# One p load for three batches, gate constants loaded one by one, and a new order of 300 steps in an attention and mixture-of-experts kernel

## Chip, cores and metric

The kernel runs on one core of a Trainium2 chip. The metric is the device time of one execution in microseconds (us). The kernel before takes 265.82 us, the median of three runs (265.61 to 266.9).

Engine names: PE does matmuls and transposes, PEld its weight loads, DVE is the vector engine, ACT the scalar engine, POOL the general one, SP the engine that issues DMA transfers (its own waits show as SPq). Each engine takes its instructions in the order in which the program lists them.

## What is computed

The reference is a chain of three stages on float32 data (4 batches, 8 heads, 576 rows, head dimension 64, 32 packed rows, 8 experts), cut here to what matters:

```python
def sm_attn(qq, kk, vv):                  # softmax(qq kk^T / 8) vv
    ...
p_packed = sm_attn(p, k, v)               # 32 rows per head attend to 576
out = sm_attn(q, p_packed, p_packed)      # 576 rows per head attend to 32
x = out.transpose(0, 2, 1, 3).reshape(2304, 512)

# MoE 1: top-1 expert by argmax(x @ w_gate), at most `capacity` = 576 rows for one expert, in row order
#   y = gate_w * (relu(x @ w1[e]) @ w2[e]) for rows that are kept, 0 for the others
# MoE 2: the same without capacity, times sigmoid(x @ w_output_gate)[e]
```

## The kernel before

**One order written out by hand.** All of the first part, from the first load to the first layer of the second MoE, is a list of 300 steps in a string, `PLAN`. The loop `for t in PLAN.split()` near the end of the kernel reads it word by word and calls the entry of `STEPS` of that name; what a step emits goes to the end of each engine's program. So `PLAN` sets one order per engine, and through SP's order the order of the loads too. A digit after a name is a batch, a piece or a half; a last letter D, A or P names the engine that copies (DVE, ACT, POOL).

**Attention, for batches b = 0 to 3.** The steps `k`, `q` (three pieces each, L283), `v` (L276) and `p` (L265) load raw rows; `dup` (L269, on POOL) copies p beside itself, since p is needed twice along the partitions. `tk` and `tq` transpose a piece with six PE transposes (tile `tp`) and copy the result out (tile `T`, L257, on ACT). `pT` (L311) does the same for p. `sa` computes the first scores (`s<-T,pT`, through the helper of L21), `ma` their negated maximum (`nb`, L332, on DVE), `ea` the exponential with its sum (L339, on ACT). `at` transposes the result in two halves (`a1T`, copied on ACT or DVE, L259), and `pp` multiplies it with v: 144 small matmuls in two parts. `sc` scales (`pps`), `pt` transposes and copies (`ppT`). The second attention works on `ppT` and q: `sb` scores (`s<-T,ppT`), `tr` a transpose in 32 x 32 blocks on DVE (L401), `mb` maximum (L409), `su` subtraction on POOL (L413), `eb` exponential, `sm` sum and reciprocal (`dn`, L420 to L422), `mu` multiplication on POOL (L426), `bk` back into `a2T` (L429).

**First gate.** Each 576 rows of x belong to one batch, and the kernel works as if all rows of a batch chose one expert; other cases have their own code behind the plan. `gg` multiplies `ppT` with the gate's weights (`gp`), `lg` makes the logits (`lp`), `lt` transposes and sums them (`Lall`, L460). For batch 0 the chain is `oa` (`mx`, `d`, L180 to L182), `ob` (`first`, `mx`, `oh`, L187 to L190: the one-hot of the expert), `rk` (rank of each row by matmuls), `kp` (which rows are kept), `cn` (counts and the expert, L211 to L226), `ei` (the cast to an integer, L236, which SP then reads with a TENSOR_LOAD, L731). Only then can the expert's weights be loaded, `wa` for w1 (L548) and `wb` for w2 (L558), 512 KB each; SP waits at the TENSOR_LOAD, and what stands behind it in its program waits too.

**Expert of batch 0 and of batches 1 to 3.** `w` multiplies a piece of w1 with `ppT`, `xh` and `xl` split x into two parts (`xl` is L571 on POOL), `h` is one of eight chunks of the first layer, `wh` and `wl` split w2, `y` is one of 32 steps of the second layer and `yo` copies its result. `lg14`, `lt14`, `oa14`, `rk14`, `kp14`, `cn14`, `rt` and `si` are the gate of batches 1 to 3 and the choice of what the second slot works on; in the second slot the same steps run on the other batches' expert. `gl`, `gt`, `gi` and `gs` are the second MoE's gate. `cst` loads the four small constants of the gates (L131 to L134), and `prep` works on them: five POOL instructions for the capacity, and a cast and a subtraction on DVE (L143, L144) that only the second gate needs.

What follows the plan (the second slot's second layer, the second MoE) is written in plain loops and is not touched.

## Time and profile before

| | |
|---|---|
| median of three runs | 265.82 us |
| the profiled execution's own time | 266.27 us |
| its span | 264.5 us |
| PE busy | 244.8 us (93%), 2529 matmuls |
| PE's weight loads | 215.2 us (81%) |
| DVE, ACT, POOL busy | 127.3, 102.9, 49.3 us (48, 39, 19%) |
| DMA | 37.17 MB, mean 141 GB/s |

The span runs from the first to the last instruction of one profiled execution. Busy time of an engine is the time that its instructions cover; PE's weight loads overlap its matmuls. An engine's idle time has a releaser, the event that ended it; "issue" means that the profile shows no event that the engine waited for. The share of DMA is the mean busy share of the core's 16 DMA engines, and PEclk is the granted clock of PE, with 1.00 for full speed.

### The profile page before, as it was taken

The numbers are of one execution on the slowest core, as the hardware profiler recorded it, in microseconds if no ns is written. First come the engines' busy times: TensorE is split into PE (matmuls) and PEld (weight loads), VectorE is DVE, ScalarE is ACT, GpSimd is POOL, SyncE is SP. The second block draws the span as 40 slices with busy tenths as digits, with TensorE's granted clock in tenths as the row PEclk, the third lists the DMA queues.
The fourth block names the chain that finished last, engine by engine and source line by source line (L and its number), as shares of the span: only waits on it lengthen the run. The fifth ranks groups of instructions, "written<-read, shape, count | busy, mean of one in ns | idle before, by whom it ended". The sixth has DMA issues, their size and how long they took to land.

```text
span 264.5 us, 6064 instructions
## 1 busy us (share of the span) xinstructions
PE 244.8 (93%) x2529; PEld 215.2 (81%) x2529; DVE 127.3 (48%) x307; ACT 102.9 (39%) x161; POOL 49.3 (19%) x70
## 2 busy tenths in 40 slices
PE   8979674979999999999999999999999999999990
PEld 6666644756797999887999999999888999988880
DVE  0227769669886343859722253495031334621000
ACT  2858666544582204464402241263231414401110
POOL 5002337053275214311600000000020000001000
PEclk9999999799999999999999999999999999999997
...
GB/s 241 362 394 388 292 403 123 54 268 137 111 79 0 2 9 321 106 315 240 119 180 158 86 100 114 0 77 239 43 46 53 108 254 0 4 0 40 62 45 47
DMA packets 29652, 37.17 MB, mean 141 GB/s; under 512 B 4144, under 2 KB 21168, under 8 KB 29616
## 3 DMA queue, kind: packets, MB, share of 16 engines
...
q8 instruction: 22, 0.36, 0.6%
q10 hardware_dynamic: 144, 0.26, 0.3%
...
HBM read 31.25 MB, written 4.72 MB: 136 GB/s over the span
## 4 chain that ended last, share of the span: by engine, by line
PE 83%; DVE 6%; issue 4%; DMA 3%; SPq 2%; ACT 0%; POOL 0%; DVEq 0%; ACTq 0%
PE h L21 27%; PE y L21 20%; PE o L21 19%; PE tp L25 4%; PE s L21 3%; DMA v<-in_v_dram 3%; PE pp L21 3%; PE l L21 2%; PE lp L21 1%; PE ppw L21 1%; SPq L283 1%; DVE oh L190 1%; PE a1Tp L25 1%; DVE d L182 1%; DVE h L614 1%
## 5 line engine op out<-in xcount | busy, mean ns | idle before, releaser
L21 PE MATMUL o<-w2bh,h 128*128 128x512 f32 x144 | 45.9, 391 | 0.0
L21 PE MATMUL y<-h,w2ah 128*128 128x288 f32 x256 | 45.0, 297 | 0.0
L21 PEld LDWEIGHTS y<-h,w2ah 128*128 128x128 f32 x256 | 37.5, 189 | 0.9 <-issue 0.9
L614 DVE SCALAR_TENSOR_TENSOR h<-h 128x576 fp32r<-128x576 f32 (+3 forms) x64 | 25.8, 447 | 25.1 <-ACT h L607 25.1
L607 ACT ACTIVATE h<-h 128x576 fp32r<-128x576 f32 x32 | 20.8, 650 | 36.5 <-PE h L21 34.0
L21 PEld LDWEIGHTS o<-w2bh,h 128*128 128x128 f32 x144 | 26.9, 188 | 5.7
L21 PE MATMUL o<-w2bl,h 128*128 128x512 f32 x80 | 31.3, 391 | 0.0
L21 PE MATMUL h<-yh,w1bh 128*128 128x288 f32 x128 | 27.5, 296 | 0.0
L21 PE MATMUL y<-h,w2al 128*128 128x288 f32 x128 | 27.4, 295 | 0.0
L21 PE MATMUL h<-yh,w1bl 128*128 128x288 f32 x128 | 27.4, 295 | 0.0
L21 PE MATMUL h<-yl,w1bh 128*128 128x288 f32 x128 | 27.3, 295 | 0.0
L725 POOL TENSOR_SCALAR osb<-osb,g 64x512 f32<-64x512 f32 x2 | 3.2, 1577 | 109.3 <-DVE osb L724 109.3
L257 ACT ACTIVATE T<-tp 128x768 f32<-128x768 f32 x24 | 19.3, 851 | 7.9 <-PE tp L25 7.7
L526 POOL TENSOR_TENSOR w2al<-wraw,w2ah 128x1024 fp32r<-128x1024 f32 x7 | 16.6, 2390 | 26.0 <-ACT w2ah L520 26.0
L21 PEld LDWEIGHTS h<-yh,w1bh 128*128 128x128 f32 x128 | 20.6, 189 | 0.2
L21 PEld LDWEIGHTS y<-h,w2al 128*128 128x128 f32 x128 | 20.6, 189 | 0.0
L21 PEld LDWEIGHTS h<-yh,w1bl 128*128 128x128 f32 x128 | 20.6, 188 | 0.0
L21 PEld LDWEIGHTS h<-yl,w1bh 128*128 128x128 f32 x128 | 20.6, 188 | 0.0
L25 PE MATMUL tp<-ident,r 128*128 128x128 f32 x144 | 19.2, 277 | 0.8 <-DMA r<-in_k_dram 0.2
L715 ACT ACTIVATE osb<-o,g 128x512 f32<-128x512 f32 (+1 forms) x8 | 5.3, 661 | 36.9 <-PE o L21 29.0
L25 PEld LDWEIGHTS tp<-ident,r 128*128 128x128 f32 x144 | 15.9, 142 | 3.6 <-issue 1.6
L21 PEld LDWEIGHTS o<-w2bl,h 128*128 128x128 f32 x80 | 15.0, 188 | 3.3
...
## 6 DMA issues: line engine op xcount, KB each, us to landing
wraw<-in_moe_w_dram SPq DMA_DIRECT2D x32, 512.0 KB, 5.4
r<-in_k_dram SPq DMA_DIRECT2D x12, 384.0 KB, 7.3
r<-in_q_dram SPq DMA_DIRECT2D x12, 384.0 KB, 8.8
...
```

The source lines that it names most:

```text
L21: return nc.tensor.matmul(out, lhsT=lhsT, rhs=rhs, start=start, stop=stop)
L25: return nc.tensor.transpose(out, in_, ident)
L182: V.tensor_tensor(d, L, bc(mx, E), op=ALU.subtract)
L190: nc.vector.tensor_tensor(oh, rev.unsqueeze(1).to_broadcast([128, n, E]), bc(mx, E), op=ALU.is_equal)
L257: nc.scalar.activation(out=o, in_=i, func=ACTF.Copy)
L283: nc.sync.dma_start(t, (k if nm == "k" else q)[b].rearrange("h (x r) d -> (h x) r d", r=R)[:, 2 * PJ * a:2 * PJ * (a + 1), :])
L526: eng.tensor_tensor(lo, src.rearrange("p a b -> p (a b)"), hi.rearrange("p a b -> p (a b)").bitcast(FP32), op=ALU.subtract)
L607: nc.scalar.activation(out=hi, in_=ps[:, :, 0:HS], func=ACTF.Relu)
L614: nc.vector.scalar_tensor_tensor(o, i, 0.0, a.bitcast(FP32), op0=ALU.max, op1=ALU.subtract)
L715: nc.scalar.activation(out=o[:n, 0:w], in_=ps[:n, 0, 0:w], func=ACTF.Copy, scale=g2[:n, t:t + 1])
L725: nc.gpsimd.tensor_scalar(o[:n], o[:n], g2[:n, t:t + 1], None, op0=ALU.mult)
```

## The change

**p.** The step `p0` loads the p of batch 0, `p1` that of batches 1 to 3 in one transfer, each into a tile of its own without room for the copy (`p_raw`, L271). `dup` still stands once for each batch and now writes both halves of `p_sb` on POOL (128 x 256 elements instead of 128 x 128, L277). The pool for it has one buffer instead of two.

**Constants.** `cst` is four steps, one load each. `prep` is two: `cap` (the five POOL instructions) and `prep` (the two on DVE). In the new order `cst0` (first gate's weights) stands ahead of `gg0`, `cst1` (capacity) and `cap` ahead of `oa01`, and `cst2`, `cst3` and `prep`, for the second gate, behind the first weight loads and between the `y` steps.

**Order.** The 300 words of `PLAN` are arranged anew. The diff shows the first line of each and the functions in full.

```diff
 PLAN = """
-warm4 warm9 warm7 k00 tk00 k01 tk01 k02 tk02 p0 dup0 pT0 k10 tk10 p1 dup1 sa00 ma00 ea00 sa01 ma01 k12 ea01 rs0 pT1
...
+k10 hn0 warm4 k00 warm9 p0 dup0 warm7 tk00 k01 tk01 pT0 k02 tk02 k22 tk10 q00 k11 sa00 ma00 k12 sa01 ma01 ea00 ea01 p1
...
@@ -127,19 +127,23 @@
     wg2r = const.tile([128, NC, 2 * E], FP32, name="wg2r")
     wg2s = const.tile([128, NC, 4 * E], FP32R, name="wg2s")
 
-    def load_consts():
-        nc.sync.dma_start(wg_sb, wg1.rearrange("(c p) e -> p c e", p=128))
-        nc.sync.dma_start(cap_i, cap.bitcast(I32).partition_broadcast(128))
-        nc.sync.dma_start(wg2r[:, :, 0:E], wg2.rearrange("(c p) e -> p c e", p=128))
-        nc.sync.dma_start(wg2r[:, :, E:], wog.rearrange("(c p) e -> p c e", p=128))
-
-    def prep_consts():
+    def load_const(i):
+        o, x = (
+            (wg_sb, wg1.rearrange("(c p) e -> p c e", p=128)),
+            (cap_i, cap.bitcast(I32).partition_broadcast(128)),
+            (wg2r[:, :, 0:E], wg2.rearrange("(c p) e -> p c e", p=128)),
+            (wg2r[:, :, E:], wog.rearrange("(c p) e -> p c e", p=128)))[i]
+        nc.sync.dma_start(o, x)
+
+    def prep_cap():
         nc.gpsimd.tensor_copy(cap2, cap_i)
         two32 = 4294967296.0
         nc.gpsimd.tensor_scalar(capf, cap2[:, 0:1], 0.0, two32, op0=ALU.is_lt, op1=ALU.mult)
         nc.gpsimd.tensor_tensor(capf, capf, cap2[:, 0:1], op=ALU.add)
         nc.gpsimd.tensor_scalar(cap2[:, 1:2], cap2[:, 1:2], two32, None, op0=ALU.mult)
         nc.gpsimd.tensor_tensor(capf, capf, cap2[:, 1:2], op=ALU.add)
+
+    def prep_gates():
         nc.vector.tensor_copy(wg2s[:, :, 0:2 * E], wg2r)
         nc.vector.tensor_tensor(
             wg2s[:, :, 2 * E:], wg2r, wg2s[:, :, 0:2 * E].bitcast(FP32), op=ALU.subtract
@@ -250,7 +254,7 @@
     sT_p = rpool("sT", 3)
     as_p = rpool("as", 2)
     ab_p = rpool("ab", 1)
-    pl_p = rpool("pl", 2)
+    pl_p = rpool("pl", 1)
 
     def evac(eng, o, i):
         if eng == 0:
@@ -261,12 +265,17 @@
     p_sb, raws, T, at = {}, {}, {}, {}
 
     def load_p(b):
-        t = pl_p.tile([128, 2, 2, D], FP32, tag="p", name="p_sb")
-        nc.sync.dma_start(t[:, :, 0, :], p[b].rearrange("h (x y) d -> (h x) y d", y=2))
+
+        n = B - b if b else 1
+        t = pl_p.tile([128, n, 2, D], FP32, tag=f"p{n}", name="p_raw")
+        nc.sync.dma_start(t, p[b:b + n].rearrange("b h (x y) d -> (h x) b y d", y=2))
+        for i in range(n):
+            raws["p", b + i] = t[:, i]
+
+    def dup_p(b):
+        t = pl_p.tile([128, 2, 2, D], FP32, tag="pp", name="p_sb")
+        nc.gpsimd.tensor_copy(t, raws.pop(("p", b)).unsqueeze(2).to_broadcast([128, 2, 2, D]))
         p_sb[b] = t
-
-    def dup_p(b):
-        nc.gpsimd.tensor_copy(p_sb[b][:, :, 1, :], p_sb[b][:, :, 0, :])
 
     PJ = 6
 
@@ -971,7 +980,7 @@
 
         STEPS = {
             "k": lambda b, a: load(b, "k", (a,)), "q": lambda b, a: load(b, "q", (a,)), "v": lambda b: load(b, "v"),
-            "p": load_p, "cst": load_consts, "prep": prep_consts, "dup": dup_p, "warm": warm,
+            "p": load_p, "cst": load_const, "cap": prep_cap, "prep": prep_gates, "dup": dup_p, "warm": warm,
 
             "pT": make_pT, "tk": lambda b, a: transp(b, "k", a), "tq": lambda b, a: transp(b, "q", a),
             "sa": s1_mm, "ma": s1_max, "ea": s1_exp, "rs": s1_rs, "at": a1_T, "pp": pp_mm, "sc": pp_scale, "pt": pp_T,
```

Three places of the new order follow. The first is the start of SP's program, the loads. Before:

```order
L283 DMA r<-in_k_dram 128x768 x3
L265 DMA p_sb<-in_p_dram 128x2x64
L283 DMA r<-in_k_dram 128x768
L265 DMA p_sb<-in_p_dram 128x2x64
L283 DMA r<-in_k_dram 128x768 x2
L283 DMA r<-in_q_dram 128x768
L276 DMA v<-in_v_dram 128x4x576
```

After:

```order
L292 DMA r<-in_k_dram 128x768 x2
L271 DMA p_raw<-in_p_dram 128x128
L292 DMA r<-in_k_dram 128x768 x3
L292 DMA r<-in_q_dram 128x768
L292 DMA r<-in_k_dram 128x768 x2
L271 DMA p_raw<-in_p_dram 128x3x128
L292 DMA r<-in_q_dram 128x768
L285 DMA v<-in_v_dram 128x4x576
```

The first two loads are now a piece of k of batch 1 and one of batch 0 (the names of the batches are not in the rows: `PLAN` has k10, k00, then p0, k01, k02, k22, then q00, then k11, k12, then p1). v of batch 0 is issued with 11 transfers ahead of it instead of 9.

The second place is the start of ACT's and PE's programs: `T` are copies of transposed k or q, `s` scores, `a` exponentials, `tp`, `pTp` and `a1Tp` PE's transposes. ACT before:

```order
L257 ACTIVATE T<-tp 128x6x8x16 x3
L311 ACTIVATE pT<-pTp 128x2x8x16
L257 ACTIVATE T<-tp 128x6x8x16
L339 ACTIVATE a_266,sm<-s,nb 128x576 x2
L311 ACTIVATE pT<-pTp 128x2x8x16
L257 ACTIVATE T<-tp 128x6x8x16 x2
L257 ACTIVATE T<-tp 128x3x128x2
L379 ACTIVATE pps<-pp,sm 128x128 x2
```

After:

```order
L261 ACTIVATE T<-tp 128x6x8x16 x2
L320 ACTIVATE pT<-pTp 128x2x8x16
L261 ACTIVATE T<-tp 128x6x8x16 x2
L348 ACTIVATE a_284,sm<-s,nb 128x576 x2
L261 ACTIVATE T<-tp 128x3x128x2
L261 ACTIVATE T<-tp 128x6x8x16 x2
L261 ACTIVATE a1T<-a1Tp 128x512
L320 ACTIVATE pT<-pTp 128x2x8x16
L261 ACTIVATE T<-tp 128x3x128x2
L348 ACTIVATE a_368,sm<-s,nb 128x576 x2
```

Ahead of the second `pT`, that of batch 1, stand now three copies of `T` and half of `a1T` behind the two exponentials. The scaling `pps` of batch 0 leaves ACT, and the exponentials of batch 1 come in its place. PE before:

```order
L25 MATMUL tp<-ident,r 128x128 x18
L25 MATMUL pTp<-ident,p_sb 128x128 x2
L25 MATMUL tp<-ident,r 128x128 x6
L21 MATMUL s<-T,pT 32x288 x16
L25 MATMUL pTp<-ident,p_sb 128x128 x2
L25 MATMUL tp<-ident,r 128x128 x12
L25 MATMUL a1Tp<-ident,a_266 128x128 x5
L25 MATMUL tp<-ident,r 128x128 x6
L25 MATMUL a1Tp<-ident,a_266 128x128 x4
L21 MATMUL pp<-v,a1T 32x64 x72
```

After:

```order
L25 MATMUL tp<-ident,r 128x128 x12
L25 MATMUL pTp<-ident,p_sb 128x128 x2
L25 MATMUL tp<-ident,r 128x128 x12
L21 MATMUL s<-T,pT 32x288 x16
L25 MATMUL tp<-ident,r 128x128 x18
L25 MATMUL a1Tp<-ident,a_284 128x128 x9
L25 MATMUL pTp<-ident,p_sb 128x128 x2
L21 MATMUL s<-T,pT 32x288 x16
L25 MATMUL tp<-ident,r 128x128 x6
L21 MATMUL pp<-v,a1T 32x64 x72
```

The second group of 16 `s` rows, the scores of batch 1, now stands ahead of `pp` of batch 0. (A row of a score or of `pp` shows as two matmuls in the trace.)

The third place is SP and DVE around the expert's index `e_i`. SP before:

```order
L283 DMA r<-in_q_dram 128x768 x3
L276 DMA v<-in_v_dram 128x4x576
L283 DMA r<-in_q_dram 128x768
L731 TENSOR_LOAD e_i
L731 ISA x2
L548 ISA
L548 DMA wraw<-in_moe_w_dram 128x4x256
```

After:

```order
L285 DMA v<-in_v_dram 128x4x576
L292 DMA r<-in_q_dram 128x768
L285 DMA v<-in_v_dram 128x4x576
L740 TENSOR_LOAD e_i
L740 ISA x2
L292 DMA r<-in_q_dram 128x768
L557 ISA
L557 DMA wraw<-in_moe_w_dram 128x4x256
```

A q piece (q32) now stands between the TENSOR_LOAD and the first weight load. DVE before:

```order
L211 TENSOR_REDUCE cnt<-cp 1x8
L219 TENSOR_REDUCE m<-cnt 1x1
L221 TENSOR_TENSOR eq<-cnt,m 1x8
L222 SCALAR_TENSOR_TENSOR eq<-eq,revv 1x8
L223 TENSOR_REDUCE pe_136<-eq 1x1
L224 TENSOR_SCALAR pe_136<-pe_136 1x1
L226 TENSOR_SCALAR ne_142<-m 1x1
L236 CAST e_i<-pe_136 1x1
L345 TENSOR_SCALAR sm<-sm 128x2
L346 RECIPROCAL sm<-sm 128x2
L440 COPY gsz_130<-gp 128x2x8
```

After:

```order
L215 TENSOR_REDUCE cnt<-cp 1x8
L223 TENSOR_REDUCE m<-cnt 1x1
L225 TENSOR_TENSOR eq<-cnt,m 1x8
L226 SCALAR_TENSOR_TENSOR eq<-eq,revv 1x8
L227 TENSOR_REDUCE pe_136<-eq 1x1
L228 TENSOR_SCALAR pe_136<-pe_136 1x1
L230 TENSOR_SCALAR ne_142<-m 1x1
L429 TENSOR_REDUCE dn_905<-sT 128x18
L430 TENSOR_SCALAR dn_905<-dn_905 128x18
L431 RECIPROCAL dn_905<-dn_905 128x18
L240 CAST e_i<-pe_136 1x1
L449 COPY gsz_130<-gp 128x2x8
```

The three instructions on `dn` (step `sm10`) now stand ahead of the cast to `e_i`, where before they came behind it.

## Rows read from the trace of the kernel before

**Rows 1.** The page, section 4: the chain that ended last, shares by engine.

```profile
PE 83%; DVE 6%; issue 4%; DMA 3%; SPq 2%; ACT 0%; POOL 0%; DVEq 0%; ACTq 0%
```

**Rows 2.** Windows: us, busy (x count) of each engine, PEclk, DMA share, GB/s.

```profile
16.90:23.70 6.80, 6.57 (x126) 4.25 (x125) 3.43 (x5) 5.48 (x11) 1.18 (x2) 1.00 1.05 384
23.70:30.20 6.50, 4.40 (x126) 3.76 (x127) 4.71 (x10) 5.24 (x10) 2.82 (x4) 1.00 1.02 327
...
51.10:58.40 7.30, 5.35 (x125) 4.37 (x126) 5.72 (x11) 4.43 (x7) 3.47 (x3) 1.00 0.87 280
58.40:62.00 3.60, 3.28 (x132) 1.70 (x131) 1.98 (x6) 2.07 (x5) 0.00 (x0) 1.00 0.08 23
62.00:258.40 196.40, 195.90 (x1429) 178.73 (x1428) 92.37 (x229) 64.08 (x93) 30.53 (x17) 1.00 0.33 103
```

**Rows 3.** Timeline, PE's stops: start, us, what, count [idle before, its releaser].

```profile
16.94 0.46 PE L21 MATMUL pp<-v,a1T 64*32 64x64 f32 x33 [1.04 <-issue]
...
30.22 0.93 PE L21 MATMUL pp<-v,a1T 64*32 64x64 f32 x70 [2.09 <-issue]
...
36.55 1.16 PE L21 MATMUL s<-T,ppT 64*32 64x288 f32 x19 [1.72 <-issue]
...
45.63 0.19 PE L21 MATMUL rk<-oh,tri 128*128 128x40 bf16 x1 [3.54 <-DVE oh L190]
...
51.13 0.26 PE L21 MATMUL gp<-wg_sb,ppT 64*32 64x8 f32 x10 [0.27 <-issue]
...
58.43 0.92 PE L21 MATMUL pp<-v,a1T 64*32 64x64 f32 x71 [1.95 <-issue]
...
61.98 0.95 PE L21 MATMUL s<-T,ppT 64*32 64x288 f32 x23 [0.29 <-issue]
```

**Rows 4.** The page, section 3: queue, packets, MB, share of 16 engines.

```profile
q8 instruction: 22, 0.36, 0.6%
```

**Rows 5.** Timeline, SP's queue: the fifth load.

```profile
2.94 0.58 SPq L283 DMA_DIRECT2D r<-in_k_dram  x1
```

**Rows 6.** DMA issues, 3 to 3.4 us: that load, KB, us to landing.

```profile
r<-in_k_dram SPq DMA_DIRECT2D x1, 384.0 KB, 5.2
```

**Rows 7.** Timeline of PE, 9 to 19 us.

```profile
9.09 1.20 PE L21 MATMUL s<-T,pT 64*32 64x288 f32 x32
...
14.57 1.32 PE L21 MATMUL pp<-v,a1T 64*32 64x64 f32 x111 [0.29 <-DMA v<-in_v_dram]
...
17.33 1.53 PE L25 MATMUL tp<-ident,r 128*128 128x128 f32 x12
```

**Rows 8.** Timeline of ACT, 10 to 15 us.

```profile
10.71 0.74 ACT L339 ACTIVATE a<-s,nb 128x576 f32<-128x576 f32 x1 [0.70 <-DVE nb L332]
...
12.15 0.38 ACT L311 ACTIVATE pT<-pTp 128x256 f32<-128x256 f32 x1
12.42 2.32 ACT L257 ACTIVATE T<-tp 128x768 f32<-128x768 f32 x3
```

**Rows 9.** Timeline of DVE, 40 to 53 us: the gate's chain.

```profile
40.72 0.28 DVE L460 TENSOR_REDUCE Lall<-lt 128x16 f32<-128x32 f32 x2
...
43.24 2.33 DVE L190 TENSOR_TENSOR oh<-rev,mx 128x40 bf16<-128x40 f32 x1
...
49.41 0.14 DVE L236 CAST e_i<-pe 1x1 int32<-1x1 f32 x1
...
51.55 0.74 DVE L420 TENSOR_REDUCE dn<-sT 128x18 f32<-128x576 f32 x1
```

**Rows 10.** Timeline of POOL, beside `oh`.

```profile
42.88 2.64 POOL L571 TENSOR_TENSOR xl<-a2T,xh 128x1152 fp32r<-128x1152 f32 x1
```

**Rows 11.** Windows: the stretch behind the wait for `oh`, columns as in rows 2.

```profile
46.50:49.50 3.00, 3.00 (x164) 2.04 (x149) 2.73 (x13) 1.65 (x4) 0.00 (x0) 0.50 0.02 5
```

**Rows 12.** Timeline, SP's queue: the first four weight loads.

```profile
50.59 2.10 SPq L548 DMA_DIRECT2D wraw<-in_moe_w_dram  x4
```

**Rows 13.** DMA issues, 52.4 to 52.6 us: the last of these.

```profile
wraw<-in_moe_w_dram SPq DMA_DIRECT2D x1, 512.0 KB, 8.5
```

More of the change, by code (lines that the diff above doesn't have):

```diff
@@ L39 @@
-rt si wb11 wa10 y000 y001 y002 y003 y030 wh03 wl03 y024 y004 y005 y006 y025 y026 y027 xh1 xl1 yo02 y031 y007 wa11 rr
-wa12 wh11 wl11 yo00 y032 y033 y034 y035 y036 w10 wb10 w11 y037 yo03 gl0 hn1 h11 h10 w12 gt wh10 h12 wl10 h13 wb12 wa13
-w13 h14 gs h16 h17 wh12 wl12 h15 zo3 wb13 wh13 wl13 gi zo2
+k10 hn0 warm4 k00 warm9 p0 dup0 warm7 tk00 k01 tk01 pT0 k02 tk02 k22 tk10 q00 k11 sa00 ma00 k12 sa01 ma01 ea00 ea01 p1
+tq00 tk11 tk12 at00D at01 dup1 pT1 sa11 sa10 ma10 q01 tq01 rs0 ea10 v0 k20 ma11 pp00 pp01 sc0 ea11 q02 q10 tq02 pt0
@@ new lines @@
+rs1 sb00 tr00 sb01 tr01 mb01 tk20 dup2 q12 k21 tk21 at10D at11D tk22 pT2 dup3 tq10 sa20 su01 eb01 k30 k32 mb00 ma20
+su00 sa21 eb00 v1 ea20 ma21 ea21 sm01 pp10 pp11 sc1 q11 tq11 tq12 sm00 pt1A tk30 mu00D bk00 cst0 gg0 sb10 mu01 bk01
+xh0 pT3 at20 lg01 tr10 mb10 rs2 k31 sb11 tr11 mb11 q21 q22 q20 tq20 q30 tk31 su10 lt01 tk32 at21 cst1 tq21 eb10 cap
+oa01 ob0 rk01 kp01 v2 q31 v3 sa30 ma30 ea30 sa31 ma31 ea31 cn01 sm10 pp20 pp21 sc2A ei su11 eb11 gg1 rs3 xl0 tq22 pt2
+q32 at30 at31 sb20 mu10 pp30 pp31 sc3A sm11 mu11 tq30 tr20 mb20 su20 bk10 bk11 sb21 tr21 gg2 eb20 sm20 tq31 tq32 mu20
@@ new lines @@
+pt3 mb21 wa03 w03 sb30 tr30 su21 eb21 bk20 mb30 sm21 mu21 h07 wa01 w01 su30 wa02 wb01 h06 sb31 cl tr31 wb02 w02 mb31
+h02 cst2 cst3 gg3 eb30 sm30 h03 su31 eb31 sm31 mu30 bk30 bk21 mu31 wh01 bk31 h04 wh02 wl02 h05 wa00 w00 lg14 h00 h01
+lt14 oa14D y030 y020 y031 wb03 cr wl01 y021 y022 ob1 rk14 kp14 y032 y033 cn14 wh03 wl03 prep y034 y035 wb00 y036 rt si
+wb11 y023 wh00 wl00D y037 y024 y025 yo03 y026 y027 yo02 xh1 rr y000 y001 wa10 wa12 wh11 y002 y010 y011 y012 y013 y014
+wa13 y003 y004 y005 y006 wl11 y007 yo00 y015 y016 w10 y017 yo01 w13 xl1 hn1 h10 h11 h17 h16 zo2 wb10 wh10 wa11 w11 zo3
@@ L42 @@
+w12 gl0 h14 gt h13 wb13 h12 wl10 h15 wh13 wb12 wh12 wl13 gi gs wl12
 """
```

9 lines of the change are left out of this document (removed).

## The prediction

> **What bounds the kernel now.** I read the chain that ended last first: 83% of it is PE work [rows 1]. The windows then say where PE is not busy: from 62.0 to 258.4 us it works 195.90 of 196.40 us [rows 2], so a new order can win at most half a microsecond there. All that can move lies in the first 62 us, the attention with the first gate.
>
> The timeline of PE shows what it waits for there. One stop is a real wait: 3.54 us before the rank product `rk`, for DVE's one-hot `oh`. The others have no releaser but "issue": 1.04, 2.09, 1.72 and 1.95 us are the large ones [rows 3]. The reader should count matmuls between them: 126, 126, and later 125 and 132 (a window's edge cuts a few) [rows 2]. The queue named "instruction" carries 22 packets with 0.36 MB in all, 16 KB each [rows 4]. My reading is that PE's program comes in pages of some 126 matmuls with their weight loads, that a page is asked for when PE enters the one before it, and that a stop is what is left of the fetch when PE is through. Two pages from 16.94 to 30.22 take 13.28 us and the next to 36.55 takes 6.33, with a DMA share over 1.0; beside the first expert's weights one takes 7.30 (51.13 to 58.43, share 0.87); at a share of 0.08 one takes 3.55, to 61.98 [rows 2, 3]. Early on, page entries and not matmuls set the pace.
>
> Here a rule speaks against the reading. The trace stops after each such page, 2.09 us at the worst [rows 3]. The Trainium skill (Runtime: NRT & Kernel Launch, Instruction fetch mechanics) says that the sequencer fetches the next 16 KiB block while it executes the current one, and that crossing into it is mostly hidden. By that rule the stops of the new order, some 7 us in my sum, would not exist and the time would be near 259 us; the trace does not agree, with 6.8 us of issue stops in four rows.
>
> **The change, part by part.** The own time of the profiled execution is 266.27 us, 1.77 over its span; the median of the three runs is 265.82, 0.45 lower. I work out the difference on the trace and put it on the median.
>
> *First loads and first scores.* k10 now goes ahead of k00. A place later it still lands while the warm-up matmuls run: nothing. But k02, with p ahead of it, is in fifth place: issued at 2.94 [rows 5], landing 5.2 us later [rows 6], at 8.1. Six transposes (0.73, half of a row of twelve without its overlapped end [rows 7]) and ACT's copy (2.32 / 3 = 0.77 [rows 8]) bring the first score to 9.8 instead of 9.09 [rows 7]: 0.7 late.
> Then ACT is the bound: its order puts three copies and half of a1T ahead of pT of batch 1, and PE's order puts the scores of batch 1 ahead of pp of batch 0. The first exponential is 10.71 - 9.09 = 1.62 after the score begins, at 11.4; both are read 1.45 later (12.15), 12.85; three copies 2.32; half of a1T 0.6 (512 columns against 768 in 0.77); pT 0.38: 16.2 [rows 8]. PE follows with those scores, 1.2, and a transposed piece, 0.73: pp begins at 18.1. v0 is a place or two later than before and there by then. In before pp began at 14.57 with that score and piece (1.9 us) not yet done [rows 7], so this stretch loses 1.6.
>
> *Pages.* Counted in the new order (a score or pp row of the order is two matmuls in the trace) the pages begin after 218, 344, 470 and 596 matmuls: half way into pp of batch 0, in a1T of batch 1, half way into pp of batch 1, at a1T of batch 2. The first is entered at 18.1 + 72 x 0.012 (1.32 / 111 [rows 7]) = 19.0, before at 16.94. PE's own work per page, summed in the same way, is some 5.5, 5.1 and 4.7 us, less than the mean of 6.54 that a page took under loads ((13.28 + 6.33) / 3), and by their sizes the loads of q, k and v run on to some 39 in the new order too. So 19.0 + 3 x 6.54 = 38.6 for the fourth page, against 36.55 [rows 3]: 2.05 late. The stops do not go; they are three of 1 to 2 us.
>
> *The gate.* From there PE needs 3.7 us (rest of a1T, `lp`, a score, two transposed pieces, `lt`) to 42.3. In before DVE took from 40.72 to 45.57 from `Lall` to the end of `oh` [rows 9], 4.85; the cast and subtraction of the second gate's constants leave this place, an estimated 0.35 (the two short reductions beside them took 0.28). The slow part stays: `oh` takes 2.33 us because POOL's `xl` of 2.64 us starts just before it [rows 9, 10], and in the new order POOL still has `d`, `su`, `xl` in this sequence. 42.4 + 4.5 = 46.9 for `rk`, 1.3 late; PE's stop shrinks from 3.54 to 2.6. After the old stop the granted clock was 0.50 from 46.5 to 49.5 [rows 11], which is 1.2 GHz; after the stops of 2.09 us no slice shows it. 2.6 is nearer to 2.09, so I take full clock: 0.6 us gained up to the next page entry (bounds 0 and 0.9).
> That entry is 46.9 + 2.5 - 0.6 = 48.8 (2.5 from `rk` to some 48.1 in before); the fetch, beside no loads, took 3.0 from there (51.13): 51.8, 0.7 late.
>
> *The expert's index and its weights.* Three DVE instructions (`dn`, 0.74 [rows 9], and two short ones, 1.2 in all) now stand before the cast to `e_i`, and one q load goes before the weights. In before the cast is at 49.41, 3.8 after `rk`, and the first weight load at 50.59 [rows 9, 12]. Now 46.9 + 3.9 - 0.5 + 1.2 = 51.5, and the first load at 52.6: after the page entry of 51.8, where before it was ahead of it (50.59 against 51.13). So this page comes in 3.0 to 3.6 us, and PE needs 4.0: next entry 55.8 instead of 58.43. The stop of 1.95 goes.
> What is late next is the page after it: it is asked for with five loads in flight (in before the last of four landed 8.5 us after its issue [rows 13]), so 6.54 rather than 3.55: 62.35, while PE's work is 4.5, to 60.3. Entry before: 61.98. From there both have the same work left up to the first y step (two halves of scores, three weight products, eight chunks, `lp`): 0.4 late in all.
>
> *The rest.* One p load of three batches in place of three saves two issues on SP, which is not waited for there; the copies on POOL grow to twice their columns, beside PE's transposes; without that cover a few tenths. After `lp` the order of y steps and chunks is new, and the second gate's logits come four chunks later; a whole layer of y steps still hides the index that they give, and PE has no wait there to lose: nothing, bounds -0.5 (all idle of rows 2) and +1.5 (a chunk's worth of waiting).
>
> Sum: +1.6 in the first stretch, +0.45 in pages, -0.75 at the gate, -0.6 clock, -3.3 for the page freed of loads, +3.0 for the one after: +0.4 us. On the profiled run 266.7, on the median 266.2.
>
> **Rivals.** (1) *Slower: pages take longer under loads.* The new list lets the loads follow each other more tightly. The row for it is 7.30 [rows 2, 3]; three such pages cost 3 x 0.76 = 2.3 more: 268.5. From 7.0 a page it decides. Against: those 7.30 came from weight loads. A smaller form: the page entered at 51.8 is caught by loads as in before, to 59.1, then 4.5 of work to 63.6, 1.25 more: 267.5. It needs the index 0.8 us earlier against the page.
> (2) *Faster: the last page is not held.* Then PE arrives at 60.3, 2.05 sooner, of which the first weights' copies take back some tenths: 264.4. For it: in before such a page beside the tail of four loads took 3.55 us. Against: five loads are issued when it is asked for.
> The Trainium skill (DMA: Bandwidth & Descriptors, Queues, rings and completion order) has a DMA engine alternate between queues packet by packet, so a page would wait for a packet and not for loads. By that rule rival 2 would hold, with 264.4, and every page under loads would take about 3.5; the trace, with 6.33 to 7.30, does not agree.
> (3) *Faster: ACT is not the bound early.* If pp of batch 0 begins at 16.6, each later milestone moves up by 1.5: 264.7. For it: the chain on ACT rests on where one load lands. Against: every link of it is a row.
>
> **How the numbers follow.** Forecast 0.42, its own range 264.8 to 267.2; rival 1 with its smaller form 0.32; rivals 2 and 3 together, each with the half microsecond of idle time, 0.26. 0.5% is 1.3 us, about what a measurement here can tell from no change: rival 1 lies above it, rivals 2 and 3 at its lower edge or, two things together, below, the forecast within. The range of 8 in 10 goes from 263.6 (half of rivals 2 and 3 together) to 268.7 (rival 1 and a little waiting late).
>
> **What would show it.** Right: the first issue stop, in pp of batch 0, gone, but pp itself beginning at 18; issue stops that end near 25.5, 32 and 38.6, in a1T and pp of batch 1 and at a1T of batch 2; the wait for `oh` at 2.6 with `oh` still over 2 us; no stop in pp of batch 3; one of 2 us in the scores of batch 3, to 62. Wrong: pp before 17, pages under loads off 6.2 to 7.0, or new idle time of PE after 82.

## The result, and the profile after

The changed kernel takes 270.36 us, the median of four runs (269.15 to 274.54), against 265.78 for the kernel before. The ratio is 1.015, with a 95% interval of 1.010 to 1.020. A second measurement beside the experiments gave 1.021 (1.015 to 1.026). Ratios leave out executions more than 1.5% above the fastest of the same kernel, and the traces of runs 4, 6, 9 and 15 come from such executions. The forecast was 266.2, no change; the change is 4.6 us slower. The profiled execution took 270.63 us of its own, with a span of 268.9, so it lost 4.36 us on the one that the prediction was worked out on.

The work is the same: the busy time of PE is 245.2 us after 244.8. The page's head and its line of busy times:

```profile
span 268.9 us, 6069 instructions
...
PE 245.2 (91%) x2529; PEld 216.5 (80%) x2529; DVE 127.6 (47%) x312; ACT 101.7 (38%) x157; POOL 48.5 (18%) x69
```

So the loss is waiting, and some work at a lower clock. The timeline of PE at its stops, in the columns of [rows 3] (start, us, what, count, the idle time before it and its releaser):

```profile
7.73 0.85 PE L25 MATMUL tp<-ident,r 128*128 128x128 f32 x6 [1.68 <-DMA r<-in_k_dram]
...
10.76 1.21 PE L21 MATMUL s<-T,pT 64*32 64x288 f32 x32 [0.25 <-ACT T L261]
...
19.05 1.65 PE L21 MATMUL pp<-v,a1T 64*32 64x64 f32 x144
...
33.33 0.96 PE L21 MATMUL pp<-v,a1T 64*32 64x64 f32 x71 [2.69 <-issue]
...
47.92 0.19 PE L21 MATMUL rk<-oh,tri 128*128 128x40 bf16 x1 [2.95 <-DVE oh L194]
...
54.09 0.23 PE L21 MATMUL gp<-wg_sb,ppT 64*32 64x8 f32 x4 [1.70 <-issue]
...
59.74 0.78 PE L21 MATMUL pp<-v,a1T 64*32 64x64 f32 x55 [1.77 <-issue]
...
90.50 0.23 PE L21 MATMUL rk<-oh,tri 128*128 128x120 bf16 x1 [0.94 <-DVE oh L194]
...
121.94 1.10 PE L21 MATMUL ppw<-wraw,pts 64*32 64x256 f32 x32 [1.00 <-DMA wraw<-in_moe_w_dram]
```

The reader is to see three kinds. The stop of 1.04 in pp of batch 0 [rows 3] is gone, as forecast; those in pp of batch 1 and pp of batch 3 are not. The wait for the first one-hot is 2.95 instead of 3.54. And two waits stand behind 82 us, for the second one-hot and for a weight load, where before had neither, only one of 0.40 us at 123 us for a split on DVE (`wl`).

The windows behind two of the stops, in the columns of [rows 2]: the clock is 0.50 behind the 2.69 us, which it was not behind the 2.09 us in the trace of before, and 0.59 and 0.56 behind the wait for the one-hot, where [rows 11] have 0.50. A trace is one execution, and the mean granted clock differs between executions of one kernel: it is 0.968 to 0.992 in the 23 executions of the kernel before beside runs 16 to 18, and 0.988 in the trace that the prediction was worked out on.

```profile
34.00:36.00 2.00, 2.00 (x38) 1.91 (x20) 1.61 (x5) 0.62 (x1) 0.00 (x0) 0.68 0.98 375
36.00:38.00 2.00, 2.00 (x11) 1.93 (x10) 1.64 (x3) 1.42 (x3) 0.00 (x0) 0.50 0.80 238
...
48.00:50.00 2.00, 2.00 (x37) 0.83 (x37) 1.75 (x7) 0.00 (x0) 0.00 (x0) 0.59 0.00 0
50.00:52.00 2.00, 2.00 (x142) 1.85 (x136) 1.63 (x9) 1.66 (x4) 0.00 (x0) 0.56 0.03 8
```

What holds the two one-hots up is seen when DVE's timeline is laid beside POOL's (`first`, `oh` and `d` are steps on the way to a one-hot). DVE first (the answers to [rows 9]):

```profile
44.14 1.14 DVE L191 SCALAR_TENSOR_TENSOR first<-d,revv 128x40 f32<-128x40 f32 x1 [0.37 <-POOL d L186]
...
45.55 2.32 DVE L194 TENSOR_TENSOR oh<-rev,mx 128x40 bf16<-128x40 f32 x1
...
87.71 1.79 DVE L186 TENSOR_TENSOR d<-Lall,mx 128x120 f32<-128x120 f32 x1
```

POOL at the same places (the answer to [rows 10] is the second):

```profile
44.07 1.16 POOL L422 TENSOR_TENSOR sT<-sT,mx 128x576 f32<-128x576 f32 x1
45.18 2.63 POOL L580 TENSOR_TENSOR xl<-a2T,xh 128x1152 fp32r<-128x1152 f32 x1
...
86.97 2.39 POOL L535 TENSOR_TENSOR w2al<-wraw,w2ah 128x1024 fp32r<-128x1024 f32 x1 [3.71 <-ACT w2ah L529]
```

Each of the three DVE instructions ends when POOL's does: 45.28 and 45.23, 47.87 and 47.81, 89.50 and 89.36. In the order before, no POOL instruction ran beside the second one-hot, and its d took 0.29.

Last, SP's queue around the weights (the answer to [rows 12]): the loads begin at 54.14, 0.05 us behind the page entry of 54.09.

```profile
54.14 0.33 SPq L292 DMA_DIRECT2D r<-in_q_dram  x1
54.68 1.55 SPq L557 DMA_DIRECT2D wraw<-in_moe_w_dram  x3
```

### The profile page after: what moved, and what is told of

Same layout as the page of the kernel before. It is cut to its first block, busy times and chain, and to the rows that moved or that the text cites. A ratio compares the mean times of both kernels' runs of the same rounds, so it can differ in the third digit from the quotient of the medians.

```text
span 268.9 us, 6069 instructions
## 1 busy us (share of the span) xinstructions
PE 245.2 (91%) x2529; PEld 216.5 (80%) x2529; DVE 127.6 (47%) x312; ACT 101.7 (38%) x157; POOL 48.5 (18%) x69
## 5 line engine op out<-in xcount | busy, mean ns | idle before, releaser
L25 PE MATMUL tp<-ident,r 128*128 128x128 f32 x144 | 20.6, 291 | 2.6 <-DMA r<-in_k_dram 2.2
L25 PEld LDWEIGHTS tp<-ident,r 128*128 128x128 f32 x144 | 17.0, 149 | 5.5 <-issue 3.0
```

The costliest lines, as they stand in the source:

```text
L25: return nc.tensor.transpose(out, in_, ident)
```

## The experiments

All ratios are to the kernel before, run beside on the same chip (266.2 to 267.3 us there), with the 95% interval. A diff of a step's place shows the words of the plan that change.

**1. The old order with the new loads** (`old_order_new_loads`).

```diff
-p2 ... p3 ... cst ... prep
+cst0 cst1 cst2 cst3 ... cap prep
```

> The order of the steps of before, with the new functions: p of batches 1 to 3 in one load where p1 stood, the four constant loads one behind the other where they stood, both halves of p copied on POOL. Theory (the order is what costs): within 0.7 us of before, 265.1 to 266.5, with the same stops of PE. Rival (the loads and copies themselves cost, for instance a p that lands later and holds the second pT): 268 to 270, with a first stop of PE at the transposes of p of batch 1.

Measured: 1.004 (1.001 to 1.007). PE's stops are those of before within 0.3 us, but for pp of batch 3 (1.13). That is a little more than the theory allowed: the loads and copies cost some quarter of the loss (0.4% of 1.5 to 2.1, and 0.7 at the end of the interval); the rest is the order.

**2. k01 ahead** (`after_k01_first`).

```diff
-k10 ... k00 ... p0 ... k01 ... k02
+k00 k01 ... p0 k02 k10
```

> The changed kernel with its first loads in the order k00, k01, p0, k02, k10; nothing else moves. In the changed kernel PE waited 1.68 us for k01, in fourth place, and its first score began at 10.76 instead of 9.09. Theory (everything behind is late because the first scores are): the score begins near 9.2, pp of batch 0 near 17.6, every later page is asked for 1.4 sooner, and the time falls by about 1.4, to 269. Rival (pages come when the stream of loads lets them): pp of batch 0 begins sooner, but the stop in pp of batch 1 ends within 0.5 of 33.3 and the time falls by less than 0.5.

Measured: 1.018 (1.012 to 1.024), no gain. The first score began at 10.55 only, since now k02, in fourth place, and then ACT's copies held it. And the first page stopped PE in pp of batch 0:

```profile
8.05 0.85 PE L25 MATMUL tp<-ident,r 128*128 128x128 f32 x6 [0.65 <-DMA r<-in_k_dram]
9.77 0.84 PE L25 MATMUL tp<-ident,r 128*128 128x128 f32 x6 [0.87 <-ACT T L261]
...
22.21 0.96 PE L21 MATMUL pp<-v,a1T 64*32 64x64 f32 x72 [2.60 <-issue]
```

Neither theory is settled by it; run 16 tries the first loads again.

**3. xl later, in the changed kernel** (`after_xl_late`).

```diff
-rs3 xl0 tq22 ... sb20 mu10 pp30
+rs3 tq22 ... sb20 mu10 xl0 pp30
```

> The changed kernel with POOL's subtraction xl moved behind its multiplication for batch 1 (mu10), so that it no longer runs beside DVE's one-hot. Theory (the one-hot is slow because of xl, and the long wait for it drops PE's clock): the one-hot takes under 0.5 instead of 2.32 us, PE's wait for it shrinks from 2.95 to about 1.1, the clock stays at 1.00 behind it (0.59 and 0.56 before), rk begins near 46.1, and the time falls by 2 to 3 us, to 267.4 to 268.4. Rival 1 (the one-hot is slow by itself): no change. Rival 2 (the next pages give it back): the one-hot is fast, but the stop at the page behind pp of batch 2 grows by as much, and the time falls by less than 0.7.

Measured: 1.010 (1.005 to 1.015). The one-hot takes 0.20 us, the wait 0.83, and the clock stays at full. PE and DVE, then the window:

```profile
45.86 0.19 PE L21 MATMUL rk<-oh,tri 128*128 128x40 bf16 x1 [0.83 <-DVE oh L194]
```

```profile
45.60 0.20 DVE L194 TENSOR_TENSOR oh<-rev,mx 128x40 bf16<-128x40 f32 x1
```

```profile
46.00:48.00 2.00, 2.00 (x106) 1.31 (x104) 1.86 (x8) 0.77 (x3) 0.00 (x0) 1.00 0.00 0
```

The gain, 0.5 and 1.0% against the two measurements of the changed kernel (1.2 and 2.8 us, for 2 to 3 expected), is clear of noise against the second alone.

**4. A third of q's bytes** (`after_q_third`): each q load takes 4 of 12 groups of rows, and the transposes read two of them over and over, so the result is not the attention of q.

```diff
-                t, (k if nm == "k" else q)[b]...[:, 2 * PJ * a:2 * PJ * (a + 1), :]
+                t[:, 0:m], (k if nm == "k" else q)[b]...[:, 2 * PJ * a:2 * PJ * a + m, :]    # m = 4 for q
```

> The changed kernel with only a third of each piece of q loaded (the transposes read the same two groups of rows three times), so that the loads of the attention carry 3 MB less; the number of loads and of PE's instructions is the same. Theory (PE's program pages wait behind the loads, and a long stop drops the clock): the stop of 2.69 us in pp of batch 1 falls below 1, the clock in the 4 us behind it is 1.00 instead of 0.5 to 0.68, lt comes 2.5 to 3.5 us sooner, and the time falls by 2 to 3.5, to 267 to 268.5. Rival (the first scores and ACT's chain set the pace): lt comes less than 1 us sooner and the time falls by less than 1.

Measured: 1.011 (1.004 to 1.018). The stop in pp of batch 1 is still 2.67 us, though the DMA share around it fell:

```profile
25.00:30.00 5.00, 4.37 (x62) 3.79 (x68) 3.27 (x6) 3.56 (x6) 1.74 (x3) 1.00 0.71 212
30.00:34.00 4.00, 1.33 (x121) 1.10 (x99) 2.43 (x5) 2.63 (x6) 2.06 (x2) 1.00 0.38 143
34.00:38.00 4.00, 4.00 (x84) 3.83 (x61) 2.99 (x7) 1.26 (x2) 0.00 (x0) 0.57 0.51 140
```

Nor does `lt` come sooner (43.11 us, 42.71 in the changed kernel). The theory in this form falls: fewer bytes alone were not seen to bring the page sooner.

**5. xl later, in the kernel before** (`before_xl_late`): the same move.

```diff
-gg1 xl0 sm11 ... mu10 bk10
+gg1 sm11 ... mu10 xl0 bk10
```

> The kernel before with POOL's subtraction xl moved behind its multiplication for batch 1 (mu10). In the changed kernel the same move cut the wait for the one-hot from 2.95 to 0.83 us and kept the clock at 1.00. Theory (xl is what makes the one-hot slow and the long wait is what drops the clock): wait for the one-hot 3.54 to about 1.4, clock 1.00 behind it, rk near 43.5; the page behind pp of batch 2 is then asked for some 2.5 us sooner, and the time falls by 2 to 3 us against before (ratio 0.989 to 0.993). Rival (the weights' loads then meet the page that is asked for at the same time and hold it): rk as sooner, but a stop in pp of batch 3 longer than 1.95, and the time falls by less than 1 us.

Measured: 0.988 (0.984 to 0.992), 263.71 us. It beats both kernels. PE's stops:

```profile
43.55 0.19 PE L21 MATMUL rk<-oh,tri 128*128 128x40 bf16 x1 [1.42 <-DVE oh L190]
...
48.85 0.26 PE L21 MATMUL gp<-wg_sb,ppT 64*32 64x8 f32 x10 [1.20 <-issue]
...
55.06 0.92 PE L21 MATMUL pp<-v,a1T 64*32 64x64 f32 x71 [0.85 <-issue]
```

The wait loses 2.12 us, the next page takes 0.93 of it back (1.20 for 0.27 [rows 3]), and the one behind it gives 1.10 (0.85 for 1.95).

**6. Head of the changed order, tail of the old** (`after_head_before_tail`).

```diff
-lg14 h00 h01 lt14 oa14D y030 ...
+h00 h01 lg14 wl01 y010 lt14 oa14D y011 ...
```

> The changed kernel up to the logits of batches 1 to 3 (w2's first quarter takes the place of its third there, with both chunks 0 and 1 ahead of the logits), and behind them the order of before. In the changed kernel PE waited 0.94 us for the second one-hot and 1.00 for a weight load at 121 us, where before had 0 and 0.40. Theory (some 1.3 of the 4.6 us are the new order behind the logits): both waits go, and the time is 1.0 to 1.6 us under the changed kernel's, ratio to before 1.009 to 1.011. Rival (these waits are slack that a later wait takes back, since the weights of the second expert come when they come): within 0.4 us of the changed kernel, ratio 1.013 to 1.016.

Measured: 1.022 (1.016 to 1.027). The wait for the second one-hot went, but two new ones came where the first chunks now follow the weights at once, so the mix says nothing on the old tail:

```profile
81.53 0.53 PE L21 MATMUL h<-xh,wh 128*128 128x288 f32 x2 [0.98 <-ACT wh L600]
...
83.48 0.85 PE L21 MATMUL h<-xh,wl 128*128 128x288 f32 x2 [1.15 <-DVE wl L601]
```

**7. Fewer buffers** (`after_qk8`).

```diff
-    qk_p = apool("qk", 12)
+    qk_p = apool("qk", 8)
```

> The changed kernel with 8 instead of 12 buffers for the raw pieces of k and q, so that fewer loads are issued ahead and fewer bytes stand in the queues when PE asks for a page of its program; bytes, instructions and orders are the same. Theory (a page waits behind the loads issued before it): the packets of the pages come 1 to 3 us after PE enters the page before, instead of 3.2 to 5.1, the stop of 2.69 us in pp of batch 1 falls below 1.5, the clock behind it stays at 1.00, and the time falls by 1 to 3 us, unless PE now waits as long for k or q. Rival (the delay of a page is set by how busy the engines are, not by what is queued): packets still 3 to 5 us late while the DMA share is 1.0, stop of 2.5 to 2.9 and half clock behind it, no gain.

Measured: 1.011 (1.005 to 1.017). The stop in pp of batch 1 is 2.67 us as it was, and the clock behind it is full this time. That is neither theory whole: the page is as late as the rival says, and a stop of that length does not always cost the clock. The page behind it then takes 4.69 us instead of 5.92, so that the half clock there cost 1.2 us in the changed kernel's trace.

```profile
34.08 0.96 PE L21 MATMUL pp<-v,a1T 64*32 64x64 f32 x71 [2.67 <-issue]
```

```profile
34.00:38.00 4.00, 3.65 (x115) 3.30 (x122) 2.78 (x7) 2.12 (x4) 0.14 (x1) 1.00 0.28 67
```

**8. 52 more instructions in the warm-up** (`after_pad26`).

```diff
+        if n == 9:
+            for _ in range(26):
+                mm(nc, ps[:, 1, 0:8], wz[:, 0:128], wz[:, 0:8], True, True)
```

> The changed kernel with 26 more matmuls of 8 columns (52 instructions) in the warm-up, while PE waits for the first loads anyway. Theory (the stops are page boundaries, one in 256 instructions): the stop in pp of batch 1 moves from behind its 73rd matmul to behind its 47th, that in gp of batch 2 back into pp of batch 2 by 26 matmuls, that in pp of batch 3 from behind its 89th to behind its 63rd; time within 1 us of the changed kernel's. Rival (the stops belong to the steps, for instance to v): they stay at the same matmuls.

Measured: 1.018 (1.011 to 1.024). The stops that are left stand at the same count of matmuls from the program's start, and so 26 matmuls earlier in the work: the one of gp of batch 2 is now in pp, 14 of whose matmuls and all of gp follow it. In pp of batch 1 and pp of batch 3 there is none, at the old place or the new. The scores and gp of batch 0 stop, which never did, also at page entries by that count, and so do the transposes behind.

```profile
25.45 0.70 PE L21 MATMUL s<-T,ppT 64*32 64x288 f32 x11 [1.90 <-issue]
...
38.01 0.21 PE L21 MATMUL gp<-wg_sb,ppT 64*32 64x8 f32 x4 [2.21 <-issue]
...
54.05 0.35 PE L21 MATMUL pp<-v,a1T 64*32 64x64 f32 x7 [0.35 <-issue]
...
64.42 0.66 PE L25 MATMUL tp<-ident,r 128*128 128x128 f32 x4 [2.82 <-issue]
```

The stops belong to places in the program, one in some 126 matmuls with their weight loads, not to steps; which of these places shows a stop differs.

**9. Work in the wait for the one-hot** (`before_warm_at_oh`).

```diff
-tq21 rk01
+tq21 warm9 warm9 warm9 rk01
```

> The kernel before with 27 matmuls on zeros (54 instructions) right ahead of the rank product, while PE waits 3.54 us for the one-hot; the wait itself and xl stay. Theory (a PE that idles for long is given half the clock behind it, at a cost): the clock from 46 to 50 us is 1.00 instead of 0.54 to 0.60, and rk stays at 45.6. What that is worth: from rk to the end of pp of batch 2 PE takes some 1.3 us less. First rival: the page that is asked for in that stretch is entered that much sooner, and 0.8 to 1.4 us of it reach the end. Second rival: the weights' loads, which do not move, take it back; under 0.4 us reach the end. The 54 instructions shift every later page boundary by 27 matmuls.

Measured: 0.995 (0.992 to 0.998). rk stays at 45.65, the clock from 46 to 50 is 1.00, and 1.4 us (0.5 to 2.2) reach the end, as the first rival says. Behind the next stop, of 2.18 us, the clock falls instead in this trace, of an execution of 268.1 us; five of the twelve executions have a mean clock of 0.994 or more, where this one has 0.985:

```profile
46.00:50.00 4.00, 2.60 (x162) 1.78 (x156) 3.39 (x17) 1.55 (x4) 0.00 (x0) 1.00 0.02 4
50.00:54.00 4.00, 3.22 (x42) 2.69 (x42) 0.89 (x3) 1.51 (x3) 0.00 (x0) 0.54 0.59 188
```

**10. Head of the old order, tail of the new** (`before_head_after_tail`), the mirror of run 6.

```diff
-lg14 wl01 y010 lt14 oa14D y011 ...
+lg14 lt14 oa14D y030 y020 y031 wb03 ...
```

> The mirror of the earlier mix: the order of before (with the new loads and functions) up to the logits of batches 1 to 3, both chunks 0 and 1 ahead of them, and behind them the changed kernel's order; w2's third quarter is loaded where before loaded its first. Theory (some 1.3 of the loss are the new order behind the logits): waits of about 0.9 us for the second one-hot and 1.0 for the weights at 120 us show up, and the time is 1.0 to 1.6 us over that of the old order with the new loads, ratio to before 1.007 to 1.011. Rival (the loss is all ahead of the logits): ratio 1.002 to 1.006.

Measured: 1.002 (0.999 to 1.005): the rival. d of the second one-hot is held there too (1.85 us), but PE reaches rk later than it is done. The weights' wait is 1.32. So the new tail has its waits behind the old head too: from 62 us on PE idles 1.85 us in this trace, 0.49 in before. In the ratios it costs nothing (1.002, and 1.004 for run 1), but their intervals leave room for some 0.7 us.

**11. Half of pp left out** (`before_pp_short`): 32 of 72 rows of the second product are not computed, so the result is another, and the kernel goes on into its general code for mixed batches; only the stretch up to the gate is read. (The flag that ends the sum moves with it.)

```diff
-        for r in range(*PARTS[i]):
+        for r in range(*PARTS[i]) if i == 0 else ():
```

> The kernel before with the second part of the product with v left out in every batch: 40 of its 72 rows stand, so 128 instructions of PE less per batch, half a page, and some 0.9 us less of PE's own work. Theory (ahead of the gate PE is paced by its program pages, 256 instructions in some 6.5 us): lt, with two batches' products ahead of it, comes a whole page sooner, by 4 to 6.5 us, as far as the loads of k and q let it. Rival (the stops hide in other waits, the work counts): lt comes 1.8 us sooner or less.

Measured, for lt alone: 34.35 against 39.24 us, 4.9 sooner, for 1.8 us of work less.

```profile
34.35 0.49 PE L25 MATMUL lt<-ident,lgT 128*128 128x128 f32 x3
```

The theory: ahead of the gate, PE is paced by the pages of its program more than by its own work.

**12. xl later, d on DVE, constants later** (`xl_late_d_on_dve`), on the kernel before.

```diff
-xh0 cst ... q31 prep ... oa01 ob0
+xh0 cst ... q31 cap ... oa01D ob0        # and xl0 behind mu10, prep ahead of cr
```

> The kernel before with xl behind mu10, the one-hot's subtraction d on DVE instead of POOL, and the cast and subtraction of the second gate's constants moved behind the y steps of chunk 1. In every row so far a DVE instruction that met a POOL subtraction ended when POOL's did: sm 0.69 to 40.66 (POOL to 40.63), first 1.14 to 43.03 (POOL to 42.97), oh 2.33 to 45.57 (POOL to 45.52). Theory (DVE is held until POOL is through): with d on DVE, POOL's second subtraction starts a us sooner and holds d until about 41.8 instead of first until 43.0; oh ends near 42.6 instead of 43.5, PE waits 0.5 instead of 1.42, and the time falls by 0.6 to 1.0 against the kernel with xl moved alone, ratio to before 0.984 to 0.987. Rival (first and oh are slow for another reason): oh ends after 43.2 and the time is that of the other, 0.988.

Measured: 0.984 (0.980 to 0.988), 263.01 us, the fastest kernel of the study. DVE and POOL:

```profile
40.88 0.69 DVE L347 TENSOR_SCALAR sm<-sm 128x2 f32<-128x2 f32 x1
...
42.24 0.48 DVE L184 TENSOR_TENSOR d<-Lall,mx 128x40 f32<-128x40 f32 x1
...
43.22 0.20 DVE L192 TENSOR_TENSOR oh<-rev,mx 128x40 bf16<-128x40 f32 x1
```

```profile
40.38 2.28 POOL L415 TENSOR_TENSOR sT<-sT,mx 128x576 f32<-128x576 f32 x2 [4.48 <-DVE mx L411]
```

POOL's two subtractions end near 41.52 and 42.66, DVE's held instructions at 41.57 and 42.72. The hold follows POOL's work wherever that goes. `oh` ends at 43.42, not at 42.6, since `lt` came 0.9 us later in this trace than in run 5; from `lt` to `rk` it is 3.27 us for 4.26. The time is the theory's, but 0.984 cannot be told from the 0.988 of run 5, and the later constants are a part of the edit.

**13. The changed kernel without the holds** (`after_no_holds`).

```diff
-oa01 ob0 ... rs3 xl0 ... ob1 rk14 kp14 ... cn14 wh03 wl03
+oa01D ob0 ... mu10 xl0 ... wh03 ob1 wl03D rk14 kp14 ... cn14
```

> The changed kernel with no POOL work beside the two one-hots: xl behind mu10, d of the first one on DVE, and the split of w2's last quarter on DVE behind the second one-hot. Theory (POOL holds DVE until it is through): the wait for the first one-hot falls from 2.95 to under 1.0, d of batches 1 to 3 from 1.79 to 0.3, the wait for the second from 0.94 to 0, and the time falls by 2 to 3 us, ratio to before 1.003 to 1.007. Rival (the second wait is there because everything ahead is late): the second wait stays over 0.6 and the ratio is that with xl moved alone, 1.010.

Measured: 0.997 (0.995 to 1.000), less than the theory's 1.003: level with the kernel before, which keeps its own hold. The wait for the first one-hot is 0.62, those for the second and for the weights at 121 us are gone, and d of the second takes 0.28. (The wait for the weights is not the hold's: with the same tail it is 1.17 and 1.43 us in runs 16 and 17.)

```profile
43.67 0.19 PE L21 MATMUL rk<-oh,tri 128*128 128x40 bf16 x1 [0.62 <-DVE oh L194]
```

```profile
82.79 0.28 DVE L186 TENSOR_TENSOR d<-Lall,mx 128x120 f32<-128x120 f32 x1
```

**14. The index one instruction later** (`after_ei_late`).

```diff
-sc2A ei su11 eb11 gg1
+sc2A su11 eb11 gg1 ei
```

> The changed kernel with the cast of the expert's index one instruction later on DVE, behind the copy of gp, so that the weights are loaded some 1.2 us later; nothing else moves. Theory (a page that is asked for just ahead of loads comes at once, one asked for with them waits): the packet of the page behind pp of batch 3 comes 1.1 to 1.3 us after the page before it is entered instead of 3.33, the stop there falls from 1.77 to under 0.5, and the chunks still find their weights; the time falls by 0.5 to 1.5 although the weights come later, ratio 1.009 to 1.013. Rival (later weights are what counts, or the page is slow in any case): the stop stays over 1.3 or PE waits for the first weights, ratio 1.015 or more.

Measured: 1.017 (1.010 to 1.023). The packet comes as expected, the gain does not. With the first load at 55.49 instead of 54.14, the packet of the page is there between 55 and 56 us; in the changed kernel it came between 57 and 58.5. The first view is of this kernel, the second of the changed one (queue, packets, MB, share):

```profile
q8 instruction: 1, 0.02, 7.2%
```

```profile
q8 instruction: 1, 0.02, 3.7%
```

The stop of 1.77 is gone and that page is entered at 57.83 instead of 59.74, but in this run's profile 0.9 us of the 1.9 are left at the end, and in the median nothing. Nor is the edit shown to be what took the stop away: in eight traces of the new order with the index where it was (runs 2 to 4, 6, 7, 13, 16 and 17) the first load is issued 0.17 to 0.82 us behind the entry, the packet comes 1.1 to 1.6 us behind it, and pp of batch 3 has no stop either.

**15. The same in the fastest version** (`best_ei_late`).

```diff
-cn01 ei pp20 wa03 ... tq22 gg1
+cn01 pp20 ... tq22 gg1 ei wa03
```

> The fastest version so far (before with xl late, d on DVE) with the cast of the index behind the copy of gp, so that its weight loads are issued some 1.5 us later, at about 49.9 instead of 48.35, behind the page entry at 48.5. Theory: the packet comes at about 49.7 instead of 52.28, the stop of 0.85 in pp of batch 3 goes, 0.5 to 0.9 us less, ratio to before 0.981 to 0.983. Rival (the weights now come too late, or the next page takes the loads' place): a wait for the first weights or a stop of the page after it, ratio 0.984 or more.

Measured: 0.996 (0.992 to 1.000), worse than 0.984, at the rival's ratio. In the trace, of an execution of 268.7 us where the median is 266.0, the first load is issued at 52.06, not at 49.9, PE waits 1.50 us for a copy of ACT, and the page behind stops it; what the other executions lose is not shown:

```profile
59.87 0.67 PE L21 MATMUL s<-T,ppT 64*32 64x288 f32 x3 [1.50 <-ACT ppT L259]
62.20 1.46 PE L21 MATMUL s<-T,ppT 64*32 64x288 f32 x23 [1.66 <-issue]
```

**16. No holds, k first** (`no_holds_k_first`).

```diff
-k10 ... k00 ... p0 ... k01 ... k02
+k00 k01 k02 p0 k10
```

> The changed kernel without the POOL holds (after_no_holds), with the loads k00, k01, k02 ahead of p0 and k10. Theory (the first loads set the start): the first score begins at 9.1 to 9.4 instead of 9.6 to 12.7, pp at 17.3, and as the pages follow from there, 0.5 to 2 us less: ratio to before 0.990 to 0.995. Rival (the fetch of the first pages waits behind the loads all the same): the score is early, the entry into the page in a1T of batch 2 stays at 38 to 39, ratio 0.996 or more.

Measured: 0.997 (0.993 to 1.001), the rival: first score at 9.59, page at a1T of batch 2 entered at 39.07.

**17. No holds, k first, pp first** (`no_holds_pp_first`).

```diff
-dup1 pT1 sa11 sa10 ma10 q01 tq01 rs0 ea10 v0 k20 ma11 pp00 pp01 sc0 ea11
+q01 tq01 rs0 v0 pp00 pp01 sc0 dup1 pT1 sa11 sa10 ma10 ea10 k20 ma11 ea11
```

> As no_holds_k_first, and pp of batch 0 ahead of the scores of batch 1, as before had it. Theory (the page entered in pp of batch 0 is asked for and entered late because pp is, and the pages behind it keep that lateness): pp begins 5.5 to 6.2 us behind the first score, at 15, page entries near 17 and 37, lt near 40, and the time is that of the old order without holds, ratio 0.984 to 0.988. Rival (it is the rest of the new order): 0.990 to 0.995, as no_holds_k_first.

Measured: 0.999 (0.994 to 1.003), neither. pp of batch 0 came no sooner, since v, with 11 transfers ahead of it, was not there:

```profile
17.94 2.14 PE L21 MATMUL pp<-v,a1T 64*32 64x64 f32 x144 [3.34 <-DMA v<-in_v_dram]
```

**18. The changed kernel again** (`after_again`).

> The changed kernel itself, beside the two: 1.012 to 1.018 if the first measurement holds; first score between 10 and 12.5, the two one-hots' waits of about 3 and 0.9 us.

Measured: 1.021 (1.015 to 1.026), above what was expected, with an interval that meets the first one's; first score at 10.70, waits of 2.96 and 0.94. Not everything comes again. The first load is issued 0.15 us behind the entry of 54.64, the packet comes 1.97 us behind it, and pp of batch 3 has no stop. Behind the stop of gp of batch 2, where the first trace has full clock, it falls to 0.50 for a while:

```profile
54.64 0.23 PE L21 MATMUL gp<-wg_sb,ppT 64*32 64x8 f32 x4 [1.81 <-issue]
```

```profile
54.00:58.00 4.00, 3.36 (x20) 3.34 (x21) 1.84 (x7) 1.22 (x3) 1.16 (x1) 0.64 0.49 144
```

## Why the prediction was wrong

Taken as one number it missed by 4.2 us. By its own sum, against the profiled execution, it missed by 3.96, and the parts of that are read from the entries of pages and rk in its one trace (an entry without a stop is found by counting matmuls). Two of its own signs of being wrong came: a page of 7.5 us, and new idle time of PE after 82.

- **First stretch and pages**: forecast +2.05 at the page entered at a1T of batch 2 (38.6), measured +2.70 (39.25). pp of batch 0 began at 19.05, not 18.1: k01, in fourth place, held the second transposes for 1.68 us, and I had looked at the fifth load alone (whose terms, 8.1, 0.73 and 0.77, add up to 9.6, not 9.8). The three pages took 19.5 us from 19.75, forecast 19.6, so rival 1 in its large form did not come. But that the mean of 6.54 came out is luck: the pages took 6.1, 7.5 and 5.9, with one stop of 2.69 for the three forecast, and the last of them is PE's own work at half clock, which takes 4.7 at full clock (runs 7 and 13).
- **The gate**: forecast -0.75, measured -0.41 (rk at 47.92, +2.29). The wait was 2.95 for 2.6.
- **The clock**: "2.6 is nearer to 2.09, so I take full clock". It fell to 0.59, and from rk to the entry of 54.09, 0.67 us were lost where 0.6 were to be gained: 1.27. Of these, 0.80 lie up to the page entry before (2.70 us for 1.9) and 0.47 in the fetch (3.47 for 3.0).
- **The page freed of loads**: "The stop of 1.95 goes." It was 1.77; the page took 5.65 us instead of 4.0, with the first load issued 0.05 us behind the entry. This is rival 1's smaller form, which I priced at 267.5. It is the chance of this trace: the second trace of the kernel and eight of its variants, with 0.15 to 0.82 us between (runs 14 and 18), have no stop there, as forecast. The page behind it was to be held for 6.54 us and took 5.19 without a stop, which gave 1.36 of the 1.65 back; in the second trace it took 6.48, with a stop of 0.99.
- **The rest**: "PE has no wait there to lose: nothing." 1.41 were lost behind the page entered in the scores of batch 3 (64.93): PE waits 0.94 for the second one-hot and 1.00 for a weight load, where before waits 0.40. This is the step that failed outright; run 18 has the same waits, 0.94 and 1.22. The first is POOL's hold on `d` (run 13). The cause of the second is open. I had the rows of the hold in hand (`oh` beside xl [rows 9, 10]), used them for the first one-hot and did not ask what POOL does beside the second.

The sum of the misses, 0.65 + 0.34 + 1.27 + 1.65 - 1.36 + 1.41, is the 3.96.

What the runs add is the weight of the holds. Without them the new order is 1.7 to 2.3% faster than with them and level with the kernel before (run 13), the old order 1.6% (run 12, with the constants later). That POOL's work makes the one-hots late is shown by taking it away at three places, and that the long wait costs the clock behind it by giving PE work in the wait (run 9). But by these ratios the holds are the smaller part of what the change cost. The old order has the first of them too, and without holds in either the new order is still 1.3% behind (0.997 and 0.984, within some 0.5%), of 1.5 to 2.1% with them.

A rule for such holds stands in the Trainium skill (SBUF — State Buffer, Who interferes with whom): a DVE instruction with both inputs in SBUF and a GpSimd instruction that reads SBUF exclude one another, as do a DVE instruction in a two-port mode and GpSimd, and the one that is issued second waits until the first is through. The trace agrees at nine places of four kernels, with ends within 0.14 us, in `sm`, `d`, `first` and `oh`; a reduce of 0.7 us that ran beside POOL kept its length. By that rule the second hold could have been suspected from the order, in which the split of w2's last quarter is POOL's next step there; that it starts ahead of the one-hot, though `PLAN` has it behind, only the times show.

What stays open is this 1.3%, the greater part of the loss. The first loads do not account for it (run 16); pp ahead of the scores was not tested cleanly, since v then decided (run 17). Part of it seems to go with the clock: the mean granted clock is 0.979 to 0.996 in the twelve executions of run 13, with the middle one at 0.983, and 0.986 to 0.995 in the six of run 12, and their two traces, at 0.996 and 0.995, span 262.0 and 261.7 us. No run shows why the clock is lower in the new order.

Why a page is late under loads is open too. In runs 4 and 7 fewer bytes stood ahead of it, and the stop was 2.67 us in both, against 2.69 and 3.28 in the two traces of the changed kernel.
